# Rounding of the output weights on VectorE, and result copies ahead of the next block's rounding

## The chip, the cores and the metric

The kernel runs on one core of one Trainium2 chip. A core has five engines that run at the same time, each in the order of its own queue: TensorE (PE in the profile), VectorE (DVE), ScalarE (ACT), GpSimd (POOL) and SyncE (SP, which here issues the DMAs). They wait for one another through semaphores. The metric is the device time of one execution in microseconds (us); lower is better.

## The reference

The kernel computes two attention layers over the same input and mixes them with a gate. The sizes are 2048 positions, 448 channels, 16 heads of 28 channels.

```python
def _A_ref(x, wqkv, wo):            # W, dil = 8, 2: each position looks at 8 earlier ones, two apart
    qkv = (x @ wqkv).reshape(B, S, 3, H, Dh)  # q, k, v
    idx = pos[:, None] - off[None, :]
    ...
    logits = jnp.einsum("bhsd,bhswd->bhsw", q, kg) * scale
    attn = _softmax(logits, axis=-1)
    o = jnp.einsum("bhsw,bhswd->bhsd", attn, vg)
    return o.reshape(B, S, D) @ wo
def _B_ref(x, wqkv, wo):            # full attention
    ...
    scores = jnp.einsum("bhqd,bhkd->bhqk", q, k) * (Dh ** -0.5)
    o = jnp.einsum("bhqk,bhkd->bhqd", _softmax(scores, axis=-1), v)
    return o.reshape(B, S, D) @ wo
g = _sigmoid((x * gate_w).sum(-1, keepdims=True))
return g * _A_ref(x, A_wqkv, A_wo) + (1 - g) * _B_ref(x, B_wqkv, B_wo)
```

## The kernel before, in words

**Split numbers.** The matmuls take a rounded float format (F32R). To keep the precision of 32 bits, a factor is split into a high part, the value rounded to that format, and a low part, the value minus the high part. A product then has three terms: high times high, high times low, low times high. A split is thus a rounding copy followed by a subtraction. In most places ScalarE rounds and VectorE or GpSimd subtracts.

**Stages.** First the projections of both layers are computed. Then comes the attention of layer B in 16 units `u` of 16 steps each: a unit is a group of four heads and a block of 512 queries, and a step `st` is one tile of 128 keys. One step on TensorE has twelve score matmuls (L979) and the product of the step before with V (L945, four matmuls, counted as eight in the trace). ScalarE takes the exponentials of the scores (L984), two instructions a step, each over the scores of two heads (128 keys, 2 x 512 queries). Until step 235 or so TensorE also computes scores ahead of time to find the maximum of each row, which VectorE reduces. Layer A is computed beside this on GpSimd and VectorE, fitted into free time by a planner.

**Hooks.** Work that belongs to a step is put on lists by `at(position, step, function)` and issued by `run(position, step)`. Within a step the positions come in this order: `pre`, the scores with `mid`, `dve`, then the planner's VectorE and ScalarE items, `act`, the product with V of the step before, `end`. An engine's instructions are executed in the order in which they are issued, so the position sets what stands in front of what.

**The output weights.** The two output matrices are stacked to seven tiles of 128 rows and 448 columns. `raw_wo` loads tile k in step 232 + k into a buffer `wor`; `split_wo` splits it in step 237 + k into a high part (L775) and a low part (L776). These parts lie in the memory of keys and queries that are no longer used (`KH`, `KL`, `QP` in the profile).

**The end of the units.** After a unit, `fin_copy` copies the accumulator `av` to `osb` (L850, ScalarE). A chain of small steps then normalises it: `fin_sum` and `fin_sum2` send the row sums through DRAM, `fin_inv` takes the reciprocal (L863, VectorE) and multiplies with the gate (GpSimd), `fin_spread` and `fin_spread2` spread the factors, `fin_on` multiplies (GpSimd), `fin_hi` and `fin_lo` split the product (ScalarE L883, GpSimd L887) and `fin_store` stores the parts to DRAM. The factors for the last unit are worked out in the output stretch, one step of this chain per output tile; `op_tile` gets them as `behind`.

**The output stretch.** The output has four blocks of 512 rows and in each four tiles of 128 rows, 16 tiles `j` in all. Tile `j` is 21 matmuls (L832): seven parts of the inner dimension, three terms each. It is accumulated in one of two banks, `accs[j % 2]`, so tile j + 2 can't start before the result of tile j has been copied out. `op_out` makes that copy, on ScalarE for even tiles (L843) and on VectorE for odd ones (L841), and issues the store. In the first two tiles of a block the parts of the next block are loaded: `op_load_a` brings four parts of layer A unsplit (`oar`), `op_load_b` the parts of layer B that were stored split. `op_split` splits the four parts of layer A (L810 on ScalarE, L811 on VectorE); they are parts 0 to 3 of the seven. For the first block this was done during the attention, with VectorE doing both halves (L808, L811).

**Buffers.** Loads, results and the parts of the last normalisation share eight buffers of one pool (`mtile`). A new one waits until an older one's last reader is done. All DMAs named here are issued by SP, in program order.

Of the kernel before, what the change touches and what calls it, by code (L numbers as in the profile page):

```python
# [10 lines left out]
AF = mybir.ActivationFunctionType  # L11
# [14 lines left out]
def gated_mix_kernel(ctx: ExitStack, tc: tile.TileContext, xT, xn, gw, wA, wB, woAB, out):  # L26
    nc = tc.nc
# [184 lines left out]
    with tc.tile_pool(name="xp", bufs=1) as xp, tc.tile_pool(name="wp", bufs=2) as wp:  # L212
# [243 lines left out]
        for n, t in enumerate(tiles):  # L456
# [4 lines left out]
            for w in splits:  # L461
                i, k = (n - splits[w][0]) * splits[w][1], splits[w][1]
# [60 lines left out]
    def at(pos, st, f):  # L523
        hooks.setdefault((st, pos), []).append(f)
# [25 lines left out]
    def reads(bank, inst):  # L550
        p, i = pair_of(bank)
        if p is not None:
            last_read.setdefault((p, i), []).append(inst.ins)
        return inst
# [16 lines left out]
    def mtile(name):  # L571
        return pm.tile([128, 512], F32, tag="M", name=name)
# [186 lines left out]
    WO_AT = OP0 + 8  # L759
# [5 lines left out]
    wo = [spare[:7], spare[7:]]  # L765
# [3 lines left out]
    def raw_wo(k):  # L769
        wor[k] = mtile("wor")  # L770
        nc.sync.dma_start(wor[k][:, :D], woAB[k])

    def split_wo(k):
        raw = wor.pop(k)[:, :D]
        nc.scalar.activation(wo[0][k], raw, AF.Copy)  # L775
        nc.vector.tensor_tensor(out=wo[1][k], in0=raw, in1=wo[0][k].bitcast(F32), op=ALU.subtract)  # L776

    def a_done(st):
# [7 lines left out]

    for k in range(7):
        at("pre", WO_AT + k, lambda k=k: raw_wo(k))
        at("act", WO_AT + 5 + k, lambda k=k: split_wo(k))

    oaT, onT, raws = {}, {}, {}

    def oa_tiles(b):
        if b not in oaT:
            oaT[b] = [[oP["2"].tile([128, 512], F32R, tag=f"oa{p}{k}", name=f"oa{p}{k}") for p in ("hi", "lo")]
                      for k in range(3)]
        return oaT[b] + [[t[0:64] for t in on_tiles(b)[0]]]

    def op_load_a(b, k):
        n = 128 if k < 3 else 64  # L800
        raws[b, k] = mtile("oar")[0:n]
        nc.sync.dma_start(raws[b, k], oa_scr[128 * k:128 * k + n, 512 * b:512 * b + 512])

    def op_split(b, k, rounded=None):
        raw = raws.pop((b, k))
        hi, lo = oa_tiles(b)[k]
        if rounded:
            rounded(hi, raw)  # L808
        else:
            nc.scalar.activation(hi, raw, AF.Copy)  # L810
        nc.vector.tensor_tensor(out=lo, in0=raw, in1=hi.bitcast(F32), op=ALU.subtract)  # L811
# [7 lines left out]
    def op_load_b(b, k, rows=128):  # L819
        r0, p0 = (0, 64) if k == 0 else (128 * k - 64, 0)  # L820
        n = 64 if k == 0 else rows
        for t, src in zip(on_tiles(b)[k], (on_hi, on_lo)):
            dma_r(t[p0:p0 + n], src[r0:r0 + n, 512 * b:512 * b + 512])
# [3 lines left out]
    def op_mm(j, bank, ks, first=False, last=False):  # L827
        b, jj = divmod(j, 4)
        for k in ks:
            for i, (a, c) in enumerate(TERMS):  # L830
                src = (oaT[b][k] if k < 3 else onT[b][k - 3])[a][:, 128 * jj:128 * jj + 128]
                writes(bank, nc.tensor.matmul(bank[:, :D], src, wo[c][k],  # L832
                                              start=(first and k == ks[0] and i == 0),
                                              stop=(last and k == ks[-1] and i == 2)))

    def op_out(j, bank, eng=0):
        t = mtile("res")

        c = D // 2 if j == NJ - 1 else 0
        if eng:  # L840
            reads(bank, nc.vector.tensor_copy(t[:, c:D], bank[:, c:D]))  # L841
        if c or not eng:
            reads(bank, nc.scalar.activation(t[:, :c or D], bank[:, :c or D], AF.Copy))  # L843
        nc.sync.dma_start(out.rearrange("(p j) c -> p j c", j=NJ)[:, j, :], t[:, :D])
# [79 lines left out]
    def op_tile(j, behind):  # L924
        bank = accs[j % 2]
        b, k = divmod(j, 4)
        if j:
            op_mm(j, bank, (0, 1), first=True)
        for i in (2 * k, 2 * k + 1) if b < 3 else ():
            if i < 4:  # L930
                op_load_a(b + 1, i)
                op_load_b(b + 1, i)
            if 2 <= i < 6:
                op_split(b + 1, i - 2)
        for f in behind:
            f()
        op_mm(j, bank, (2, 3, 4, 5, 6) if j else (3, 4, 5, 6), last=True)
        op_out(j, bank, j % 2)

    prev = None  # L940

# [52 lines left out]
    for u in range(NU):  # L994
        g, b = divmod(u, NB)
# [51 lines left out]
    for j in range(NJ):  # L1047
        op_tile(j, steps[j] if j < len(steps) else ())
# [25 lines left out]
```

## Time and profile before

| | |
|---|---|
| median of three runs | 906.94 us (906.22 to 907.09) |
| the profiled execution | 906.91 us |
| its span | 905.1 us |
| TensorE busy | 896.3 us, 99% |
| VectorE busy | 734.6 us, 81% |
| ScalarE busy | 646.9 us, 71% |
| GpSimd busy | 640.7 us, 71% |
| granted TensorE clock | 1.0 |

How to read what follows. In a row of the timeline stand the start in us from the start of the span, the time it took, the engine, the line of the kernel, the operation, the output and its inputs by the program's names, shapes, and how many such instructions are merged; the bracket at the end says how long the engine was idle before it and what ended the idle time. PEld is the loading of weights into TensorE, which overlaps the matmuls. A row of the chain that ended last has a start, a time and what the end of the program waited for in that time. In a row of windows stand the stretch, its length, and for each engine its busy time and instructions, then the granted clock, the mean share of the DMA engines that is busy, and GB/s. TensorE's matmuls are pipelined and their ends are modelled, so its busy share says little about how fast it goes. The time between the start of one matmul and of the next says more.

### The profile page before, as it was taken

How to read it: one execution, taken by the hardware profiler on the slowest of the kernel's cores; microseconds unless marked ns; L12 is line 12 of the kernel's file. 1: busy time of each engine (PE TensorE's matmuls, PEld its weight loads, DVE VectorE, ACT ScalarE, POOL GpSimd, SP SyncE). 2: the span in 40 equal slices, each digit the busy share in tenths (PEclk: the TensorE clock that was granted, in tenths of full speed). 3: DMA queues.
4: the chain of work that ended last, by engine and by line, in shares of the span. 5: the costliest groups of instructions: out<-in, count | busy, mean ns of one | idle time of the engine just before them, and what ended most of it. 6: DMA issues, size and time to landing. Idle time of an engine off the chain costs nothing.

```text
span 905.1 us, 20549 instructions
## 1 busy us (share of the span) xinstructions
PE 896.3 (99%) x8326; PEld 539.4 (60%) x8326; DVE 734.6 (81%) x954; ACT 646.9 (71%) x777; POOL 640.7 (71%) x507
## 2 busy tenths in 40 slices
PE   9999999999999999999999999999999999999998
PEld 6799999999954444444444444444444444334987
DVE  6488999999979999999999999999999999721220
ACT  6456434343378888988988989889889898997220
POOL 2389847464469689999999999999999689401000
PEclk9999999999999999999999999999999999999999
DMA  9876503449373241225224242352221222245781
GB/s 266 283 250 189 170 12 84 133 123 115 106 254 73 94 129 49 71 51 159 70 57 145 81 116 76 76 136 61 61 61 27 79 55 50 81 101 150 224 265 62
DMA packets 116758, 105.04 MB, mean 116 GB/s; under 512 B 77192, under 2 KB 84744, under 8 KB 115880
## 3 DMA queue, kind: packets, MB, share of 16 engines
q1 hardware_dynamic: 116520, 103.47, 41.8%
q8 instruction: 65, 1.06, 0.5%
q10 hardware_dynamic: 144, 0.26, 0.1%
q14 instruction: 29, 0.24, 0.1%
HBM read 62.72 MB, written 40.96 MB: 115 GB/s over the span
## 4 chain that ended last, share of the span: by engine, by line
PE 93%; DMA 3%; ACT 2%; SPq 1%; DVE 0%; issue 0%; ACTq 0%
PE T L979 30%; PE av L945 27%; PE r L304 15%; PE T L832 6%; PE r L299 6%; PE r L142 4%; PE T L142 4%; ACT P L984 1%; DMA V<-in_xT 1%; DMA onlo<-on_lo 1%; DMA out<-res 0%; DMA qk_hi<-qkh 0%; DMA KH<-qk_hi 0%; SPq L99 0%; ACT KH L775 0%
## 5 line engine op out<-in xcount | busy, mean ns | idle before, releaser
L984 ACT ACTIVATE P<-T 128x1024 f32<-128x1024 f32 x512 | 497.2, 1026 | 59.1 <-PE T L979 57.7
L148 DVE TENSOR_REDUCE MX<-T 128x1 f32<-128x512 f32 x470 | 442.3, 954 | 33.9 <-PE T L142 16.9
L945 PE MATMUL av<-P,V 128*32 128x512 f32 x2048 | 272.7, 605 | 0.9 <-ACT osb L850 0.9
L979 PEld LDWEIGHTS T<-QH,KH 30*128 30x128 f32 x1024 | 92.9, 181 | 231.7 <-ACT P L984 198.3
L142 PE MATMUL T<-KH,QP 28*128 28x512 f32 x704 | 220.0, 456 | 0.1
L979 PE MATMUL T<-QH,KH 30*128 30x512 f32 x1024 | 214.1, 489 | 0.2 <-ACT P L984 0.2
L164 DVE TENSOR_REDUCE MX<-r 128x2 f32<-128x1024 f32 x160 | 192.2, 1221 | 25.7 <-PE r L142 23.9
L979 PE MATMUL T<-QH,KL 28*128 28x512 f32 x1024 | 187.7, 395 | 0.0
L979 PE MATMUL T<-QL,KH 28*128 28x512 f32 x1024 | 186.1, 393 | 0.0
L609 POOL TENSOR_TENSOR prod<-qt,kt 128x896 f32<-128x896 f32 x64 | 135.4, 2115 | 4.7 <-DMA kt<-a_scr 4.6
L367 ACT ACTIVATE raw<-r 128x896 f32<-128x896 f32 (+1 forms) x64 | 58.9, 921 | 97.5 <-PE r L304 95.3
L670 POOL TENSOR_TENSOR oat<-oat,prod 128x896 f32<-128x896 f32 x48 | 101.3, 2111 | 2.0
L142 PEld LDWEIGHTS T<-KH,QP 28*128 28x128 f32 x704 | 86.0, 181 | 27.4 <-ACT P L984 18.7
L368 POOL TENSOR_TENSOR ast<-raw 128x448 f32<-128x448 f32 x48 | 55.4, 1155 | 58.5 <-ACT raw L367 49.0
L665 POOL TENSOR_TENSOR prod<-vt,L 128x896 f32<-128x896 f32 x56 | 95.4, 1704 | 0.2
L979 PEld LDWEIGHTS T<-QL,KH 28*128 28x128 f32 x1024 | 94.3, 184 | 0.0
L979 PEld LDWEIGHTS T<-QH,KL 28*128 28x128 f32 x1024 | 93.9, 183 | 0.7
L945 PEld LDWEIGHTS av<-P,V 128*32 128x32 f32 x2048 | 40.3, 108 | 78.4 <-issue 65.2
L304 PE MATMUL r<-wh,xh 64*128 64x448 f32 (+1 forms) x512 | 82.4, 363 | 0.0
L142 PE MATMUL r<-KH,QP 64*128 64x512 f32 x320 | 80.6, 393 | 1.4 <-DMA KH<-qk_hi 1.2
L304 PE MATMUL r<-wh,xl 64*128 64x448 f32 (+1 forms) x384 | 70.1, 364 | 0.0
L614 POOL TENSOR_TENSOR prod<-prod 128x448 f32<-128x448 f32 x64 | 65.6, 1026 | 5.0
(112 smaller groups left out, 1077.6 us busy)
## 6 DMA issues: line engine op xcount, KB each, us to landing
a_scr<-ast SPq DMA_DIRECT2D x24, 448.0 KB
qk_hi<-qkh SPq DMA_DIRECT2D x24, 256.0 KB
qk_lo<-qkh SPq DMA_DIRECT2D x24, 256.0 KB
rbc<-rs SPq DMA_DIRECT2D x64, 64.0 KB
QP<-qk_hi SPq DMA_DIRECT2D x64, 56.0 KB
KL<-qk_lo SPq DMA_DIRECT2D x16, 224.0 KB
QH<-qk_hi SPq DMA_DIRECT2D x64, 56.0 KB
QL<-qk_lo SPq DMA_DIRECT2D x64, 56.0 KB
```

The lines of the kernel that those rows point to most:

```text
L142: nc.tensor.matmul(bank, qhis[u][h % 2][r, 128 * qs:128 * qs + 128], KH[u // NB % 3][r, 512 * kc:512 * kc + 512], start=True, stop=True)
L148: i = nc.vector.tensor_reduce(MX[:, n % NMX:n % NMX + k], bank, axis=X, op=ALU.max)
L164: nc.vector.tensor_reduce(m, PM[k], axis=X, op=ALU.max)
L304: nc.tensor.matmul(bank[:, 0:cols], x, ws[c][rows, k, 0:cols], start=first, stop=last)
L367: nc.scalar.activation(raw[:, :, 0:cols], PJ[n % 2][:, :, 0:cols], AF.Copy)
L609: nc.gpsimd.tensor_tensor(out=p, in0=qt[c], in1=kvt["k", c % 2][:, HALO - DIL * w:HALO - DIL * w + NJ, :], op=ALU.mult)
L614: nc.gpsimd.tensor_tensor(out=lo, in0=lo, in1=hi, op=ALU.add)
L665: nc.gpsimd.tensor_tensor(out=dst.rearrange("p j (h d) -> p j h d", d=DH), in0=kvt["v", c % 2][:, HALO - DIL * w:HALO - DIL * w + NJ, :].r ...
L670: nc.gpsimd.tensor_tensor(out=ows[c % 2][:, :, 0:56] if w == W - 1 else oat[c], in0=oat[c], in1=oat[c, w], op=ALU.add)
L945: nc.tensor.matmul(av[32 * h:32 * h + 32, :], V[:, kt, 4 * g + h, :], tiles_[h], start=(kt == 0), stop=(kt == NJ - 1), skip_group_check=True)
L979: nc.tensor.matmul(bank[a], (KH[g % 3], KH[g % 3], KL[g % 2])[t][r, ks], (qh, ql, qh)[t][r, :], start=(t == 0), stop=(t == 2))
L984: e = nc.scalar.activation(p, one if a == "2" else mine, AF.Exp, scale=SCALE).ins
```

## The change

Two things are moved. The rounding copy of `split_wo` is issued to VectorE in place of ScalarE, and the seven splits are issued at the position `dve` of their steps, not at `act`. In the output stretch `op_tile` issues the splits of the next block's parts after the tile's own result copy, no longer before the tile's second group of matmuls; they stay in the same tile (parts 0 and 1 in the second tile of a block, parts 2 and 3 in the third), and behind the step of the normalisation that `behind` holds.

```diff
     def split_wo(k):
         raw = wor.pop(k)[:, :D]
-        nc.scalar.activation(wo[0][k], raw, AF.Copy)
+        nc.vector.tensor_copy(wo[0][k], raw)
         nc.vector.tensor_tensor(out=wo[1][k], in0=raw, in1=wo[0][k].bitcast(F32), op=ALU.subtract)
...
         at("pre", WO_AT + k, lambda k=k: raw_wo(k))
-        at("act", WO_AT + 5 + k, lambda k=k: split_wo(k))
+        at("dve", WO_AT + 5 + k, lambda k=k: split_wo(k))
...
             if i < 4:
                 op_load_a(b + 1, i)
                 op_load_b(b + 1, i)
-            if 2 <= i < 6:
-                op_split(b + 1, i - 2)
         for f in behind:
             f()
         op_mm(j, bank, (2, 3, 4, 5, 6) if j else (3, 4, 5, 6), last=True)
         op_out(j, bank, j % 2)
+        for i in (2 * k - 2, 2 * k - 1) if b < 3 else ():
+            if 0 <= i < 4:
+                op_split(b + 1, i)
```

## The prediction

> **What bounds the kernel now.** I read the page first, for its span and its engine table.
>
> ```profile
> span 905.1 us, 20549 instructions
> PE 896.3 (99%) x8326; PEld 539.4 (60%) x8326; DVE 734.6 (81%) x954; ACT 646.9 (71%) x777; POOL 640.7 (71%) x507
> ```
>
> The profiled execution took 906.91 us, 905.1 of it span, 1.81 around it; the median of the runs is 906.94, so the sum below is made against 906.91 and stands for the median too. TensorE is "busy" 99% of the span, but its ends are modelled, so that row cannot tell where it is held back. I therefore read the chain that ended last, in order of time, over the two stretches that the change touches.
>
> ```profile
> 789.34 3.69 ACT P L984 x4
> 793.03 0.46 ACT KH L775
> 793.50 1.83 ACT P L984 x2
> ...
> 799.91 0.46 ACT KH L775
> 800.38 0.50 ACT osb L850
> ...
> 861.86 4.38 DMA out<-res
> 866.25 0.53 ACT res L843
> 866.78 0.04 issue
> 866.83 34.50 PE T L832 x168
> ```
>
> Two things are to be seen. From 789 to 801 the chain runs on ScalarE: two exponentials a step, and the rounding of one output weight (L775) between the steps, 0.46 us each. And at 866 it leaves TensorE a second time for a result copy (L843). Third, I read the busy times of single steps of the attention, cut where a step's first score matmul starts.
>
> ```profile
> core 0: us, PE busy (x) PEld busy (x) DVE busy (x) ACT busy (x) POOL busy (x), PEclk, DMA share, GB/s
> ...
> 796.37:798.67 2.30, 2.30 (x25) 0.84 (x21) 0.63 (x2) 2.30 (x4) 0.00 (x0) 1.00 0.92 259
> 798.67:801.91 3.24, 2.34 (x24) 0.83 (x20) 0.70 (x2) 3.24 (x6) 0.00 (x0) 1.00 0.67 129
> 801.91:803.81 1.90, 1.90 (x24) 0.66 (x20) 0.62 (x1) 1.90 (x3) 0.00 (x0) 1.00 0.48 112
> ...
> 810.62:830.60 19.98, 19.98 (x204) 7.60 (x200) 4.46 (x8) 19.18 (x21) 1.74 (x2) 1.00 0.53 152
> 792.22:810.62 18.40, 17.50 (x164) 6.32 (x161) 4.63 (x8) 18.40 (x25) 1.50 (x2) 1.00 0.45 100
> ```
>
> The last row holds eight steps, seven of them with a weight's rounding: ScalarE is busy all 18.40 us of it. The row above it holds ten steps with none: 19.98 us, 2.00 a step, ScalarE 19.18. The granted clock is 1.00 in all. So the roundings make a step that TensorE would do in 2.00 into one of 2.30.
>
> Last, the timeline where the output stretch stalls.
>
> ```profile
> 865.71 0.63 ACT L810 ACTIVATE onhi<-oar 64x512 fp32r<-64x512 f32 x1 [1.64 <-DMA on_hi<-onhi]
> ...
> 865.91 0.37 PE L832 MATMUL T<-KH,onlo 128*128 128x448 f32 x1
> 866.25 0.52 ACT L843 ACTIVATE res<-T 128x448 f32<-128x448 f32 x1
> 866.38 0.68 DVE L811 TENSOR_TENSOR onlo<-oar,onhi 64x512 fp32r<-64x512 f32 x1 [1.58 <-ACT onhi L810]
> ...
> 866.83 0.68 PE L832 MATMUL T<-KH,oahi 128*128 128x448 f32 x2 [0.55 <-ACT res L843]
> ```
>
> ScalarE stood waiting for a load until 865.71, rounded the fourth part of block 2 (L810), and only then copied result 6 (866.25), which had been complete since the end of tile 6. Tile 8 needs that bank and started at 866.83.
>
> **The change, part by part.**
>
> *Seven roundings leave ScalarE.* They are 7 x 0.46 = 3.2 us of ScalarE. Not all of it comes back, because TensorE's own 2.00 a step is the next limit. Eight steps at 2.00 are 16.0 us instead of 18.40, which would give 2.4. But one of the eight also holds the copy of the accumulator (osb, 0.50 in the chain), and it stays. Today it lengthens its step and the next to 3.24 + 1.90 = 5.14, against 2 x 2.30: 0.54. Without the roundings ScalarE has a little air that can take some of it:
>
> ```profile
> 811.64 3.83 ACT L984 ACTIVATE P<-T 128x1024 f32<-128x1024 f32 x4 [0.20 <-PE T L979]
> 815.64 3.84 ACT L984 ACTIVATE P<-T 128x1024 f32<-128x1024 f32 x4 [0.17 <-PE T L979]
> ```
>
> 0.17 us idle in two steps, so osb costs between 0.54 - 0.17 = 0.37 and 0.54. The stretch becomes 16.4 to 16.5 us, a gain of 1.9 to 2.0. One thing may take a bit of it: the last block's scores need two rows of QH that a DMA brings.
>
> ```profile
> 796.37 0.18 PEld L979 LDWEIGHTS T<-QH,KH 30*128 30x128 f32 x2 [0.84 <-DMA QH<-nm]
> ```
>
> TensorE would be there about 0.2 earlier (by my count of the two steps before), and the row says only that the DMA landed by 796.37. If it landed just then, 0.2 is lost. I take 1.9, the nearest to the step rows. Bounds: 1.6 (all small losses together) and 3.2 (every rounding comes back).
>
> *Seven copies come to VectorE.* The nearest rows are the same cast of a wider tile, and the subtraction that stands behind each copy already:
>
> ```profile
> L808 DVE CAST oahi<-oar x3: 428/428/428, 816.8 to 822.0; 128x512 fp32r<-128x512 f32 x3
> ```
>
> ```profile
> L776 DVE TENSOR_TENSOR KL<-wor,KH x4: 626/626/626, 795.8 to 803.2; 128x448 fp32r<-128x448 f32 x4
> ```
>
> At most 0.43 each (448 columns, not 512), 3.0 us in all, in a stretch where VectorE is busy 4.63 of 18.40. I take nothing on the path. The cover is VectorE's idle time; the row maxima of the scores are over by then, and the first reader of the weights is the output product, which starts where the ten-step row ends, at 830.60. Each copy waits for its weight's load, as ScalarE's rounding did; behind the last copies in VectorE's queue stands only the reciprocal of block 2's sums (L863), which itself waits for a DMA. Could it be worse than nothing? Only if a copy held a step's exponentials, and those wait for TensorE and not for VectorE. Better than nothing: no, it is already counted.
>
> *Results are copied ahead of the rounding.* The stall: the matmul before it started at 865.91, and the start-to-start distance there is 0.20, so tile 8 could have started at 866.11; it started at 866.83. Gain 0.72. Other result copies also stand behind a rounding or a subtraction today, but the bank is wanted only a whole tile later, and no other tile start has an idle time, so they give nothing on TensorE.
>
> *Roundings are now behind the result copies, and behind the steps that normalise the last block.* What is late next? A tile is 21 matmuls:
>
> ```profile
> 844.74 0.57 PE L832 MATMUL T<-KH,oahi 128*128 128x448 f32 x2
> ...
> 849.01 0.57 PE L832 MATMUL T<-KH,oahi 128*128 128x448 f32 x2
> ```
>
> 4.27 us a tile, 0.203 a matmul; the fourth part (parts 0 to 3, three matmuls each) is read 9 x 0.203 = 1.83 after the start of the block. In times of the kernel before: block 2 would start at 866.11 and read its fourth part at 867.94. That part's load lets ScalarE start at 865.71 in the worst case, as today, and its subtraction begins 0.67 later, at 866.38, and is done at 867.06: 0.9 to spare. For block 1, the reciprocal moves ahead of two subtractions:
>
> ```profile
> 842.83 0.43 SPq L859 DMA_DIRECT2D fsum<-rs  x1
> ```
>
> ```profile
> 847.70 0.68 DVE L811 TENSOR_TENSOR onlo<-oar,onhi 64x512 fp32r<-64x512 f32 x1 [2.67 <-ACT onhi L810]
> 848.34 0.25 DVE L863 RECIPROCAL finv<-fsum 128x16 f32<-128x16 f32 x1
> ```
>
> It waits for fsum, which landed somewhere between its issue at 842.83 and 848.34. At the late end the two subtractions follow at 848.6 and 849.2 and are done at 849.9, and block 1, starting at 849.01, reads its fourth part at 850.84: 0.9 to spare. Both ends cost nothing. I expect the late end, since the part that was loaded just before it let its subtraction start only at 847.70. For block 3 the two last parts now wait for result 10:
>
> ```profile
> 881.19 0.63 ACT L810 ACTIVATE onhi<-oar 64x512 fp32r<-64x512 f32 x1 [2.42 <-DMA oar<-oa_scr]
> ```
>
> Tile 10 ends at 866.11 + 3 x 4.27 = 878.9, before this load is there, and the part is read at 866.11 + 4 x 4.27 + 1.83 = 885.0; done by 882.6 or so. Nothing.
>
> The Trainium skill, "DMA: Bandwidth & Descriptors", section "Anatomy of one DMA", has a transfer cost about 2.0 us beside its bytes. By it fsum would be there at 844.8 and the reciprocal would move by 3.5 us; the sum stays 904.3, but the loads of block 2, which queue behind its result, would start as much earlier, and the second rival below would fall to 0.05. The rows just quoted, with loads let go later than that, make me leave it at its chance.
>
> *Queues.* SP's order of issues doesn't change: a split issues no DMA, and each result's store keeps its place. The eight shared buffers of loads, results and parts are freed one copy later than today for the loads; that may change which buffer a result takes, and so what it waits for (a rival below). POOL gains no instruction.
>
> **Sum:** 906.91 - 1.9 - 0.72 = 904.29, so 904.3 us.
>
> **The rivals.**
>
> 1. *ScalarE stays the pace, at its own rate.* The chain has two exponentials in 1.83. Eight steps would be 8 x 1.83 + 0.50 = 15.1, a gain of 3.3 for 1.9, and 902.9 us. Against it: ten steps without a rounding took 19.98, with ScalarE idle now and then behind TensorE. The Trainium skill, "ScalarE: Activation LUTs", section "What ACT_TABLE_LOAD costs", gives an activation without pointer operands 186 ns + 0.833 per column, less 93 where two follow each other; by that, as an estimate, an exponential is 0.946 and eight steps with osb 15.6, which would make 903.4. Chance 0.03.
>
> 2. *The stall stays.* Result 6 takes a buffer whose store isn't done, or a part comes late. The chain has a store of a result landing 4.38 us after its issue, at 866.24, just when result 6 was copied. If result 6 waits for such a store, its copy stands where it stood, and 0.72 is not gained: 906.91 - 1.9 = 905.0. For it: the stores are issued among saturated loads. Against: the copy follows the rounding in front of it by 0.54 (865.71 to 866.25), less than that rounding's own 0.63, so ScalarE's order alone explains its start. Chance 0.15.
>
> 3. *The roundings were not the limit.* The steps stay near 2.30 because something else paces them, and only the stall goes: 906.91 - 0.72 = 906.2. Against it is the ten-step row. Chance 0.08.
>
> 4. *Slower.* Result 6 waits for the store of result 5, and that store lands late. Tile 8 starts 0.58 after the landing (866.25 to 866.83 today), and the two roundings of block 2 that now stand behind result 6 move with it. Up to a landing at 866.25, in today's times, this is rival 2; from there each microsecond is lost whole: 905.0 + (landing - 866.25). It equals the median at 868.2 and is slower by 0.2% (908.75) from 870.0, when the store takes 8.1 us and not 4.38. For it: the roundings lose their place ahead of the copy, so nothing can run while it waits. Against: result 5 is copied earlier than today, so its store is issued no later. Chance 0.09.
>
> **How the numbers follow.** Forecast 0.65, rivals 0.03, 0.15, 0.08, 0.09. A measurement of this kernel tells about 0.2%, 1.81 us, from no change, so faster means below 905.13. The forecast's own range is 903.7 to 904.7 (gains of 1.6 to 2.5 in the attention, with 0.72). Faster: 0.65 + 0.03 + 0.06, since rival 2 lies on the border; same: 0.09 + 0.08; slower 0.09. The range must leave out no more than 0.2: rival 1, rival 3 and rival 4, so it runs from 903.4 to 905.7.
>
> **What would show it.** Right: no ScalarE instruction at the weights' rounding line; eight steps in about 16.5 us where 18.40 were; the start of the output stretch 1.9 earlier; no idle time of TensorE before tile 8; result 6 copied within 0.6 of the end of tile 6. Wrong: steps that stay at 2.30; an idle TensorE before tile 8, 4 or 12 that waits for a subtraction or a copy; result 6 that starts long after tile 6 with ScalarE idle before it; VectorE's copies much longer than 0.43.

## The result, and the profile after

The changed kernel takes 903.93 us (median of 8 runs, 903.52 to 905.54) beside 906.78 for the kernel before (8 runs). The ratio is 0.9971, with a 95% interval of 0.996 to 0.9982. It is faster, by about three tenths of a per cent; 904.3 us was forecast. The profiled execution took 903.91 us. Of all executions reported here one was slow, at a granted clock of 0.655 (the last kernel below, 1177.04 us beside 904.0 to 905.31 of its other four); its ratio leaves it out. From the page of the changed kernel:

```profile
span 902.1 us, 20546 instructions
PE 895.1 (99%) x8326; PEld 539.3 (60%) x8326; DVE 737.1 (82%) x961; ACT 644.3 (71%) x770; POOL 640.5 (71%) x507
```

ScalarE has seven instructions less (770 for 777) and VectorE seven more (961 for 954). To see where the 3.0 us between the two spans lie, I cut both traces at the same instructions: where the product with V (L945 before, L946 after) starts that is issued in step 237, in step 246 and in step 256 (steps counted from 0), and at the end. The windows of the kernel before:

```profile
791.22:811.52 20.30, 19.40 (x182) 6.97 (x180) 4.63 (x8) 20.21 (x26) 1.50 (x2) 1.00 0.43 98
811.52:832.63 21.11, 21.11 (x201) 8.72 (x197) 4.46 (x8) 19.66 (x21) 2.58 (x2) 1.00 0.55 155
832.63:905.08 72.45, 68.14 (x336) 61.40 (x335) 12.90 (x21) 13.09 (x23) 2.82 (x3) 1.00 0.59 179
```

and of the changed kernel:

```profile
790.58:809.41 18.83, 18.02 (x183) 6.78 (x181) 5.06 (x11) 17.61 (x19) 0.00 (x1) 1.00 0.47 105
809.41:830.51 21.10, 21.10 (x202) 8.69 (x198) 4.46 (x8) 19.76 (x21) 2.80 (x3) 1.00 0.55 156
830.51:902.12 71.61, 67.85 (x336) 61.45 (x335) 12.44 (x21) 13.19 (x23) 3.13 (x3) 0.99 0.59 181
```

The steps with the roundings got 1.47 us shorter, the ten steps behind them stayed, and the output stretch got 0.84 shorter. That is 2.32 with the 0.01 between. The other 0.64 stands ahead of all three windows (791.22 against 790.58). It is there from the first product with V on, as the rows of that line show (the two times ahead of the semicolon are the first and the last start, in us), first of the kernel before and then of the changed one:

```profile
L945 PE MATMUL av<-P,V x2048: 592/605/617, 259.2 to 833.1; 128*32 128x512 f32 x187
```

```profile
L946 PE MATMUL av<-P,V x2048: 592/605/617, 258.5 to 831.0; 128*32 128x512 f32 x187
```

The change touches nothing ahead of it, and a second profile of the same changed kernel (below) has 260.2 in this place. So 0.7 us lie within what the start differs from one execution to the next, and I count them as no effect of the change.

In the forecast's stretch the chain of waits of the changed kernel has left ScalarE, but for one place:

```profile
791.52 1.92 SPq L99
793.49 0.54 SPq L99
794.08 1.90 DMA QH<-nm
796.02 1.08 PE T L980 x12
797.10 1.04 PE av L946 x8
798.16 0.80 ACT P L985
798.97 0.50 ACT osb L850
...
831.57 66.81 PE T L832 x327
```

From 796.02 on TensorE is in the chain step by step; ScalarE comes only where the accumulator is copied (osb, with the exponential ahead of it). Ahead of 796.02 stand SP's issues and a load, QH<-nm. The last row says that the output runs without a break from 831.57. The timeline at the place where tile 8 used to wait:

```profile
860.57 1.29 POOL L887 TENSOR_TENSOR onlo<-on,onhi 128x512 fp32r<-128x512 f32 x1 [6.81 <-issue]
...
861.89 0.55 ACT L843 ACTIVATE res<-T 128x448 f32<-128x448 f32 x1 [3.93 <-POOL onlo L887]
...
863.78 0.37 PE L832 MATMUL T<-KH,onlo 128*128 128x448 f32 x1
...
863.99 0.57 PE L832 MATMUL T<-KH,oahi 128*128 128x448 f32 x2
864.08 0.63 ACT L810 ACTIVATE onhi<-oar 64x512 fp32r<-64x512 f32 x1 [1.12 <-DMA oar<-oa_scr]
...
864.40 0.37 PE L832 MATMUL T<-KH,oalo 128*128 128x448 f32 x1
...
864.74 0.68 DVE L811 TENSOR_TENSOR onlo<-oar,onhi 64x512 fp32r<-64x512 f32 x1 [1.06 <-ACT onhi L810]
```

Tile 8 starts at 863.99, 0.21 behind the matmul before it; before, the distance was 0.92. Result 6 is copied at 861.89, the rounding of the fourth part comes behind it at 864.08.

### The profile page after: what moved, and what is told of

The parts are those of the page before. It is cut to its first block, busy times and chain, and to the rows that moved or that the text cites. A ratio compares the mean times of both kernels' runs of the same rounds, so it can differ in the third digit from the quotient of the medians.

```text
span 902.1 us, 20546 instructions
## 1 busy us (share of the span) xinstructions
PE 895.1 (99%) x8326; PEld 539.3 (60%) x8326; DVE 737.1 (82%) x961; ACT 644.3 (71%) x770; POOL 640.5 (71%) x507
## 3 DMA queue, kind: packets, MB, share of 16 engines
q8 instruction: 65, 1.06, 0.5%
## 5 line engine op out<-in xcount | busy, mean ns | idle before, releaser
L946 PE MATMUL av<-P,V 128*32 128x512 f32 x2048 | 272.7, 605 | 0.4 <-ACT osb L850 0.4
L946 PEld LDWEIGHTS av<-P,V 128*32 128x32 f32 x2048 | 40.3, 108 | 77.8 <-issue 65.3
```

The lines of the kernel that those rows point to most:

```text
L946: nc.tensor.matmul(av[32 * h:32 * h + 32, :], V[:, kt, 4 * g + h, :], tiles_[h], start=(kt == 0), stop=(kt == NJ - 1), skip_group_check=True)
```

## The experiments

The theory was the forecast's: two independent gains, the roundings' time on ScalarE and the stall ahead of tile 8. Each kernel was timed beside the kernel before on its chip; ratios are to that. The windows have the forecast's columns: the stretch, its length, the busy time of PE, PEld, DVE, ACT and POOL, the granted clock, the DMA share and GB/s.

**One half alone: the weights.** Only `split_wo` and its hook are changed.

```diff
-        nc.scalar.activation(wo[0][k], raw, AF.Copy)
+        nc.vector.tensor_copy(wo[0][k], raw)
...
-        at("act", WO_AT + 5 + k, lambda k=k: split_wo(k))
+        at("dve", WO_AT + 5 + k, lambda k=k: split_wo(k))
```

> The first part of the change alone: the seven weights are rounded by VectorE, the splits of the output stretch stay ahead of the result copies. My theory (ScalarE paced these steps, TensorE's 2.0 us a step takes over): the stretch from the step before the first rounding to the first output matmul falls by about 1.5 us, from 38.4 to 36.9, the stall ahead of tile 8 stays at about 0.7 to 0.8, and the time falls by 1.5 us, ratio 0.9983. Rival (the whole gain of the change comes from this part, the stall being an accident of one execution): 2.3 to 2.9 us, ratio 0.997. Rival (the gain is in the output order): no change.

Measured: 906.3 us, ratio 0.9987 (0.9977 to 0.9998). The windows of this kernel, and then its timeline at tile 8:

```profile
794.87:813.35 18.48, 18.04 (x183) 6.82 (x181) 4.95 (x11) 17.65 (x19) 0.11 (x1) 1.00 0.48 108
...
834.39:906.96 72.57, 68.14 (x336) 61.38 (x335) 12.85 (x21) 13.07 (x23) 2.81 (x3) 1.00 0.60 179
```

```profile
867.60 0.63 ACT L810 ACTIVATE onhi<-oar 64x512 fp32r<-64x512 f32 x1 [1.52 <-DMA oar<-oa_scr]
...
868.14 0.52 ACT L843 ACTIVATE res<-T 128x448 f32<-128x448 f32 x1
...
868.71 0.68 PE L832 MATMUL T<-KH,oahi 128*128 128x448 f32 x2 [0.67 <-ACT res L843]
...
869.22 0.37 PE L832 MATMUL T<-KH,oalo 128*128 128x448 f32 x1
```

The stretch is 1.82 shorter (20.30 to 18.48). The stall stays and even grows, from 0.92 to 1.04 between the two matmuls, because the load in front of the rounding did not come earlier by as much as TensorE did: counted from the start of the last window, the rounding began at 33.08 before and at 33.21 here. So the first half is worth 1.82 where it acts, more than the 1.5 expected, and 1.77 over the three windows (113.86 to 112.09).

**The other half alone: the order in the output stretch.** Only `op_tile` is changed.

```diff
-            if 2 <= i < 6:
-                op_split(b + 1, i - 2)
...
         op_out(j, bank, j % 2)
+        for i in (2 * k - 2, 2 * k - 1) if b < 3 else ():
+            if 0 <= i < 4:
+                op_split(b + 1, i)
```

> The second part alone: the next block's splits stand behind the result copy, the weights are still rounded by ScalarE. My theory: the stall ahead of tile 8 goes, 0.72 of idle time and 0.10 that the first two matmuls behind it were longer, so the time falls by 0.8 us, ratio 0.9991; the attention stretch stays at 38.4. Rival (a store or a late part brings a new wait): an idle time at tile 4, 8 or 12, and no gain. Rival (the two parts are not independent, because the loads of block 2 move too): more than 1.2 us or less than 0.4.

Measured: 907.5 us, ratio 0.9996 (0.9987 to 1.0004). Its windows:

```profile
792.68:812.97 20.29, 19.39 (x183) 6.97 (x181) 4.64 (x8) 20.21 (x26) 1.50 (x2) 1.00 0.45 98
...
834.06:905.68 71.62, 67.86 (x336) 61.47 (x335) 12.63 (x21) 13.19 (x23) 3.12 (x3) 0.99 0.59 181
```

The attention is as before, the output stretch 0.83 shorter. The time alone can't show that: 0.83 us is 0.0009, and the interval reaches as far on either side. The windows of the trace do. The two halves add up: 1.82 and 0.83 here, 1.47 (and 1.91 in a second profile, below) and 0.84 together.

**One split moved.** Of all the splits only the one in front of result 6, part 3 of block 2, is put behind its result copy.

```diff
-            if 2 <= i < 6:
+            if 2 <= i < 6 and (b, i) != (1, 5):
                 op_split(b + 1, i - 2)
...
         op_out(j, bank, j % 2)
+        if j == 6:
+            op_split(2, 3)
```

> Of the twelve splits in the output stretch only one, the fourth part of block 2, is put behind the result copy of tile 6; all else is the kernel before. My theory: that one order is the whole stall, so this gains the same 0.8 us as all twelve, ratio 0.9991, with result 6 copied within 0.6 of the end of tile 6. Rival (the other splits ahead of the copies, or the steps of the normalisation that they hold back, share in it): a rest of the stall, 0.2 us or more, stays.

Measured: 907.08 us, ratio 0.999 (0.9982 to 0.9999). Its last window:

```profile
832.62:904.25 71.63, 67.86 (x336) 61.47 (x335) 12.97 (x21) 13.07 (x23) 2.81 (x3) 0.99 0.60 181
```

71.63 against 71.62 and 71.61: in these executions this one split carries all that the new order gives, and the rest of the reordering is worth nothing on TensorE. It also settles whose wait the stall was. The chain of the kernel before has a store's landing at 866.24 just ahead of result 6. Here the copy starts at 863.24, right behind the rounding in front of it (862.70), and no store holds it, so it was ScalarE's order. It comes 1.4 us after the end of tile 6, not within the 0.6 expected, since that other rounding still stands ahead of it; tile 8 starts at 866.10 and loses nothing.

**The suspected cost doubled: two roundings on ScalarE.** The kernel before, with each weight rounded twice by ScalarE into the same tile.

```diff
         nc.scalar.activation(wo[0][k], raw, AF.Copy)
+        nc.scalar.activation(wo[0][k], raw, AF.Copy)
```

> The kernel before with each of the seven weights rounded twice on ScalarE, the second time over the first. My theory: ScalarE paces these steps with nothing to spare, so seven more roundings at 0.46 us cost 3.2 us, ratio 1.0035, and a step with two takes 2.76. Rival (something else paces them, ScalarE only follows): less than 1.5 us.

Measured: 913.26 us, ratio 1.0058 (1.0045 to 1.0071). The first window, and then ScalarE's timeline in it:

```profile
792.21:817.17 24.96, 21.21 (x183) 7.17 (x181) 4.54 (x8) 24.36 (x33) 1.51 (x2) 0.93 0.35 80
```

```profile
797.89 1.92 ACT L985 ACTIVATE P<-T 128x1024 f32<-128x1024 f32 x2
799.70 0.58 ACT L775 ACTIVATE KH<-wor 128x448 fp32r<-128x448 f32 x1
800.31 0.58 ACT L776 ACTIVATE KH<-wor 128x448 fp32r<-128x448 f32 x1
800.79 1.92 ACT L985 ACTIVATE P<-T 128x1024 f32<-128x1024 f32 x2
```

The direction is as expected, and the loss is larger, 4.66 in the stretch for 3.2. A second rounding costs 0.61 and not 0.46 to 0.48: it starts 0.03 after the end of the first one (799.70 + 0.58), whose tile it writes again, while the exponential behind it starts 0.48 after its predecessor. Seven times 0.61 are 4.3. Most of the last 0.4 goes with the granted clock of TensorE, 0.93 in this window and 1.00 in that of the kernel before. The rows are from TensorE's timeline, from ScalarE's, and from the windows, for the stretch at the lower clock alone:

```profile
804.32 1.53 PE L946 MATMUL av<-P,V 128*32 128x512 f32 x8 [1.51 <-ACT osb L851]
```

```profile
807.47 1.94 ACT L985 ACTIVATE P<-T 128x1024 f32<-128x1024 f32 x2 [0.30 <-PE T L980]
```

```profile
804.79:808.20 3.41, 3.41 (x24) 1.04 (x20) 0.63 (x1) 3.08 (x5) 0.00 (x0) 0.50 0.49 79
```

TensorE waited 1.51 for osb; from 804.79 its clock was half for 3.41 us, its product with V took 1.53 where the others take 1.06, and ScalarE in turn waited 0.30 for scores. What it shows is the direction of the limit: with its roundings ScalarE sets the step, so more of them lengthen it in full.

The output stretch of this execution is 0.77 longer too (73.22 for 72.45). Tiles 4 and 7 start 0.49 and 0.56 behind the matmul ahead of them, where 0.20 is the pace, and tile 8 again 0.85. Result 2 was copied at 854.34 behind a rounding that waited for its load until 853.80, result 5 at 867.54 behind a subtraction (866.93). So the other places of the old order can stall as well, when their loads come late.

**VectorE's copies doubled.** The changed kernel, with each weight copied twice by VectorE.

```diff
         nc.vector.tensor_copy(wo[0][k], raw)
+        nc.vector.tensor_copy(wo[0][k], raw)
```

> The changed kernel, with each of the seven copies of an output weight done twice on VectorE, so 7 x 0.37 = 2.6 us more of VectorE in the stretch in which it has room. Theory (the copies are wholly hidden on VectorE, nothing reads the weights until the output product): no change, the stretch from step 237 to 246 takes 18.4 to 18.9, the end as before, ratio within 0.001 of the changed kernel. Rival (some of the changed kernel's shortfall in the attention comes from VectorE's own copies, by what they hold up): the stretch grows by 0.3 or more, ratio 0.9975 or above.

Measured: 904.86 us, ratio 0.996 (0.9947 to 0.9972); the changed kernel, timed beside it, has 0.996 too. Its first window:

```profile
791.80:810.17 18.37, 17.94 (x183) 6.75 (x181) 7.79 (x18) 17.63 (x19) 0.22 (x1) 1.00 0.48 108
```

VectorE is busy 7.79 for 5.06 and the stretch does not notice. The same doubling that cost 4.66 us on ScalarE costs nothing on VectorE.

**The changed kernel once more.** Since its first profile gave 1.47 of the forecast's 1.9, it was profiled and timed again.

> The changed kernel unchanged, timed beside these runs on the same chip: 0.9971 of the kernel before, within the interval that its first timing gave (0.996 to 0.9982); the stretch from step 237 to 246 in 18.4 to 18.9, depending on how late QH<-nm is issued.

Measured: 905.19 us beside 908.26 for the kernel before, ratio 0.996 (0.9947 to 0.9974). Its windows:

```profile
792.30:810.69 18.39, 17.94 (x183) 6.76 (x181) 4.68 (x10) 17.62 (x19) 0.00 (x0) 1.00 0.48 107
...
831.77:903.40 71.63, 67.86 (x336) 61.46 (x335) 12.63 (x21) 13.20 (x23) 3.12 (x3) 1.00 0.60 181
```

Now the stretch has all of the gain, 1.91. The difference between the two profiles of one kernel, 0.44, is in the main one wait. In the first profile TensorE waits for the load of two rows of QH at step 240:

```profile
796.02 0.60 PE L980 MATMUL T<-QH,KH 30*128 30x512 f32 x4 [0.37 <-DMA QH<-nm]
```

In the second its timeline has no wait of TensorE there:

```profile
796.30 1.06 PE L946 MATMUL av<-P,V 128*32 128x512 f32 x8
797.29 0.51 PE L980 MATMUL T<-QH,KH 30*128 30x512 f32 x4
...
800.78 1.06 PE L946 MATMUL av<-P,V 128*32 128x512 f32 x8 [0.45 <-ACT osb L850]
```

**The load of QH taken out of the way.** The changed kernel, with the last unit's parts of QH and QL loaded four steps earlier, so that SP has only the rows of `nm` left to issue when they are ready.

```diff
+            if kt == 8 and u + 2 == NU:
+                load_q_parts(u + 1)
             if kt == 12 and u + 1 < NU:
                 load_q(u + 1)
```

(`load_q` then loads the parts only where that has not been done.)

> The changed kernel, with the last unit's two parts of QH and QL loaded four steps earlier, so that only the 30 rows of nm are loaded where all three were. In the changed kernel's profile the stretch from the first av group of step 237 to that of step 246 took 18.83 us, and TensorE waited 0.37 in it for the load QH<-nm. Theory (the part of the forecast's gain that did not come was lost to that load, which stood behind another issue on SP): the wait is gone, the stretch takes 18.4 to 18.5, everything behind it as in the changed kernel (39.5 from step 237 to step 256, 71.6 from there to the end), 903.5 us against 903.9, ratio to the kernel before 0.9967. Rival (ScalarE is the limit there anyhow: the wait only moves into its queue): the stretch stays at 18.8, ratio 0.9971. Second rival (the load still comes late, since the nm rows wait as long on SP): a wait of 0.3 or more for QH<-nm remains.

Measured: 905.55 us, ratio 0.9965 (0.9952 to 0.9977). Its first window:

```profile
792.41:810.77 18.36, 17.93 (x182) 6.74 (x180) 4.95 (x11) 17.60 (x19) 0.23 (x1) 1.00 0.43 92
```

The wait is gone and the stretch is 18.36, as the theory has it. But the unchanged order reaches 18.39 when its load is in time, and the two times are alike (0.9965 and 0.996). So the wait accounts for the shortfall of the one profile; as an improvement the edit has not shown a gain.

**The place of the roundings.** The changed kernel with the hook where it stood, among ScalarE's items (`act`); the copy stays on VectorE.

```diff
-        at("dve", WO_AT + 5 + k, lambda k=k: split_wo(k))
+        at("act", WO_AT + 5 + k, lambda k=k: split_wo(k))
```

> The changed kernel, with the weights' roundings (on VectorE) written at the place where they stood before, among ScalarE's hooks, instead of among VectorE's. Theory (the engine matters and not the place, since VectorE has room in this stretch): as the changed kernel, 18.4 to 18.8 us from step 237 to step 246 (18.83 and 18.39 in its two profiles, by how late QH<-nm was issued), 71.6 behind step 256, ratio within 0.001 of it. Rival (the place has a part in the gain, through the order of VectorE's or POOL's work): 19.2 or more, ratio 0.998 or above.

Measured: 903.95 us beside 907.46, ratio 0.9964 (0.9951 to 0.9976). Its first window:

```profile
790.61:808.98 18.37, 17.93 (x182) 6.72 (x181) 4.96 (x11) 17.65 (x19) 0.22 (x1) 1.00 0.47 108
```

It is the engine and not the place.

**What is left on ScalarE: osb.** The changed kernel, with the accumulator's copy of the last unit but one on VectorE.

```diff
-        nc.scalar.activation(t, av, AF.Copy)
+        if u == NU - 2:
+            nc.vector.tensor_copy(t, av)
+        else:
+            nc.scalar.activation(t, av, AF.Copy)
```

> The changed kernel, with the accumulator's copy of the last unit but one (osb, L850) on VectorE, and nothing else. Theory (the forecast's term for osb: it is ScalarE's extra work that lengthens its step): in the changed kernel's second profile the stretch from step 237 to step 246 took 18.39, of which two steps with osb 2.58 + 1.90, against 2.10 + 1.90 for a pair without; so the stretch takes 17.9 to 18.0 (18.3 to 18.4 if QH<-nm comes late), 0.4 to 0.5 less than the changed kernel's, which is a ratio lower by 0.0005. Rival (VectorE holds up the first av matmul as long as ScalarE did): 18.4 or more with no wait for QH<-nm.

Measured: 904.69 us, ratio 0.9967 (0.9955 to 0.998). Its first window, and then its timeline at the load of QH:

```profile
792.08:810.29 18.21, 18.07 (x183) 6.96 (x181) 5.28 (x11) 17.32 (x19) 0.00 (x0) 1.00 0.48 109
```

```profile
797.30 0.29 PEld L983 LDWEIGHTS T<-QH,KH 30*128 30x128 f32 x4 [1.05 <-DMA QH<-nm]
```

The stretch is 18.21, between the two cases of the expectation, since the load came late in this execution and step 240 took 2.22 for 1.90 (counted from the starts of the products with V). The two steps that hold osb took 1.99 and 2.00, where the changed kernel's second profile has 2.58 and 1.90: 0.49 less. So osb does cost TensorE that much on ScalarE; in the time it can't be seen.

**Both, and one more rounding.** The kernel with the early load, with osb on VectorE, and beside them one rounding of a normalised block (`fin_hi` of unit 13) on VectorE.

```diff
+        if u == NU - 3:
+            nc.vector.tensor_copy(fin["hi"], fin["on"])
+        else:
+            nc.scalar.activation(fin["hi"], fin["on"], AF.Copy)
```

> The kernel early_q, and beside it the copy of the accumulator of the last unit but one (osb, 0.50 on ScalarE) and one rounding of a normalised block (the one of unit 13) on VectorE. Theory (ScalarE's extra work beside the two exponentials of a step is what lengthens steps 237 to 246): a further 0.4 goes with osb, so the stretch from step 237 to 246 takes 18.0 to 18.1, ten steps behind it hardly change (21.1, as TensorE sets 2.00 a step there) except for the one with the rounding (0.2 to 0.35 less where that falls into them), 903.0 us, ratio 0.996. Rival (osb on VectorE costs TensorE as much, since its first av matmul waits for VectorE, which has other work): the stretch is 18.4 or more, ratio 0.9967 or above.

Measured: 904.43 us beside 905.19 for the changed kernel on the same chip; ratio to the kernel before 0.9955 (0.9941 to 0.9968) beside 0.996 (0.9947 to 0.9974). Its first window:

```profile
791.55:809.62 18.07, 18.07 (x185) 6.94 (x181) 6.33 (x14) 17.45 (x19) 0.22 (x1) 1.00 0.43 93
```

The stretch is 18.07, as expected, and TensorE is busy all of it, with 2.01 a step over the nine steps. That rounding fell one step ahead of the window, not behind it as I had it: the step up to 237 took 1.90 for 2.34. The median is the lowest of the four kernels timed together, but the intervals overlap, so that it beats the changed kernel is likely and not shown.

## Why the prediction was right, point by point

**Seven roundings leave ScalarE, 1.9.** The place and the size hold: 1.91 in the second profile, 1.93 with the other hook, 1.94 with the early load, 1.82 with this half alone. The reading that gave it, two window rows of the same loop with a rounding and without, was right: with the roundings gone TensorE sets the step. Osb was put at 0.37 to 0.54 and costs 0.49.

In the first profile the gain was 1.47. The step that was mis-sized for this execution is "If it landed just then, 0.2 is lost": it is 0.44 of the stretch. The row in the kernel before that named the load (0.84 us idle of PEld until QH<-nm) was the right one. In the two profiles with the wait, TensorE went on 2.53 and 2.50 us after the first issue of that load (793.49 to 796.02 here, 794.80 to 797.30 with osb on VectorE); in the second profile it came 2.65 after it (794.64 to 797.29) and had no wait. So what counts is when SP issues the load, and that is not fixed: SP's last issue of QL<-qk_lo in front of it took 1.92 us here, while most issues ahead of it in the chain took 0.38. All four issues of QL took 3.21 us in this profile, 2.69 in the second, 3.08 in the kernel with osb on VectorE, where the wait came back, and 1.67 in the two with the doubled copies and the other hook. Why that varies from execution to execution is open.

**Seven copies come to VectorE, nothing.** Right: a copy took 0.35 to 0.40 (at most 0.43 was forecast), VectorE's stretch stays mostly idle (5.06 busy of 18.83), and doubling them changes nothing.

**Results ahead of the rounding, 0.72.** Right, with 0.84 in the profile. 0.72 are the distance between the matmuls, 0.92 to 0.20. Another 0.10 are in the two matmuls behind the stall: from their start to the third matmul it is 0.51 in a kernel with the stall (868.71 to 869.22) and 0.41 without (863.99 to 864.40). The forecast read the stall's price only up to the start. That the other reordered copies give nothing beside it is shown by the kernel with one split moved. The forecast's reason, that no other tile start had an idle time, holds for the executions of the kernel before and not for every one: with the doubled roundings tiles 4 and 7 waited too.

**What is late next.** The margins were put too wide, and still sufficed. For block 2's fourth part 0.9 was forecast: ScalarE got its load at 864.08, 1.63 earlier than before (865.71), while tile 8 came 2.12 earlier than the forecast's time for it (866.11 to 863.99). The subtraction is done at 865.42 and the part is read at 863.99 + 1.83 = 865.82: 0.4 to spare. For block 1 the late end came true, as this timeline of VectorE shows:

```profile
846.60 0.25 DVE L863 RECIPROCAL finv<-fsum 128x16 f32<-128x16 f32 x1 [6.15 <-DMA fsum<-rs]
846.77 0.63 DVE L811 TENSOR_TENSOR oalo<-oar,oahi 128x512 fp32r<-128x512 f32 x1
847.32 0.70 DVE L811 TENSOR_TENSOR onlo<-oar,onhi 64x512 fp32r<-64x512 f32 x1
```

The two subtractions are done at 848.02; block 1 starts at 846.88 and reads the part at 848.71: 0.7 to spare, for the 0.9 put down. The reciprocal came 1.74 us earlier than before (848.34), block 1 on TensorE 2.13 (849.01). For block 3 the subtraction was done at 880.79 and the part read at 882.92: 2.1 to spare, where the forecast's times leave 2.4. The Trainium skill, "DMA: Bandwidth & Descriptors", section "Anatomy of one DMA", has about 2 us beside the bytes for a transfer, fitted to those that GpSimd issues; by it, as an estimate, fsum, which SP issued at 841.15 in the changed kernel, would have been there at 843.2 or so. It let go at 846.60, 5.4 after its issue, so that figure does not hold for this load. In the forecast it would have changed only the second rival's chance.

**Rivals.** The first fell: by ScalarE's own rate nine steps with osb would take 9 x 1.83 + 0.50 = 17.0, and they never came under 18.36; once osb was gone too, they stood at 2.01 a step with TensorE busy throughout. The second did not come true, but came nearest, and here a sign of being wrong that the forecast names did show: result 6 did not come "within 0.6 of the end of tile 6" but 2.17 after it (859.72 to 861.89), with ScalarE idle before it. Its row names no store but GpSimd's onlo of the last block (860.57 + 1.29 = 861.86). The copy reads only the accumulator, so I take the wait to be for the shared buffer that it is given, and have not tested it. The copy is done at 862.44, 1.55 ahead of tile 8, so nothing is lost. With the new order alone the same copy came at 866.16 and named the same releaser. The third fell by the windows, and of the fourth there is nothing to see.

**The sum.** The sum gave 904.29, and the profiled execution took 903.91. That the two are so near is partly luck: the late load took 0.44 from the gain, and an earlier start of the attention, which has nothing to do with the change, gave 0.64. The second profile has the change's own gain without either: 1.91 + 0.82 and 0.03 between, 2.76 for the 2.62 forecast, and 0.997 of 906.9, which both intervals of the changed kernel hold.

## What to carry to other kernels

Read the price of an instruction on a pacing engine from two window rows of the same loop, with it and without it, and not from its duration: 3.2 us of rounding were worth 1.9, because the next engine's rate took over, and the wrong engine twice over cost 4.66 where the right one cost nothing. An engine's order matters at the one instruction that somebody waits for; find it in the chain, since moving it alone gave the whole gain of the reordering (0.82 of 0.83), and test the releaser that the chain names, since here it named a store and the cause was the order on ScalarE. When a gain of a few us is compared between two profiles, cut both at the same instructions first: here 0.7 of 3.0 us lay ahead of everything that was changed.

## What the runs showed of the hardware that was not expected

VectorE can stand still inside an instruction beside GpSimd. In the changed kernel's first profile a subtraction of a weight took 1.59 us, where the others of its kind take 0.63; the first row is GpSimd's, and the two are from its timelines:

```profile
788.77 1.29 POOL L887 TENSOR_TENSOR onlo<-on,onhi 128x512 fp32r<-128x512 f32 x1 [2.31 <-ACT onhi L883]
```

```profile
788.96 1.59 DVE L776 TENSOR_TENSOR KL<-wor,KH 128x448 fp32r<-128x448 f32 x1
...
790.89 0.63 DVE L776 TENSOR_TENSOR KL<-wor,KH 128x448 fp32r<-128x448 f32 x1
```

It starts 0.19 behind GpSimd's instruction and ends 0.49 behind its end. In the kernel with the doubled copies it hit a copy in the same way, 1.38 us for 0.39. It comes back in every profile with the copies on VectorE: one instruction of a split, beside GpSimd's onlo, at 1.59 to 1.63 (a subtraction) or at 1.38 and 1.39 (a copy). The Trainium skill, "SBUF — State Buffer", section "Who interferes with whom", has the two engines share a pair of ports that one instruction holds to its end; the rows agree. Here it cost nothing, since nobody waited for VectorE.

A stall of TensorE cost 0.10 us more than its length, in the two matmuls behind it (0.51 to the third matmul for 0.41). The attention began between 258.4 and 260.5 us (its first product with V) in eleven of the twelve profiles of these kernels, none of which changes anything ahead of that; this spread of 2.1 us is most of the size of the change. The twelfth, with the weights alone, began at 262.3. Its granted clock was 0.50 from 39.4 to 42.8; an estimate from these times is that this cost up to 1.7 us. In the kernel with the doubled roundings the clock was 0.50 for as long, 3.41 us, behind a wait of TensorE of 1.51 us.
